# Narrowing float64 weights on chip: the low part as 16-bit integers behind the absolute values, and the first transposed copy between two quarters

## The chip, the cores and the metric

The kernel runs on one core of one Trainium2 chip. The metric is the device time of one execution in microseconds (us); the figure to be forecast is the median of several executions.

## The reference, cut to what matters

```python
def _attn_ref(q, k, v, g_norm):                 # q, k, v: (8, 8, 576, 64) float32
    kv = np.einsum('bhsd,bhse->bhde', k, v)
    out = np.einsum('bhsd,bhde->bhse', q, kv)
    rms = np.sqrt(np.mean(out * out, axis=-1, keepdims=True) + 1e-06)
    return (out / rms * g_norm).astype(np.float32)

def _moe_ref(x, w1, w2, w3, w_out):             # x: (4608, 512)
    a = x @ w1                                  # w1, w2: (512, 1024)
    b = x @ w2
    h = a * b @ w3                              # w3: (1024, 1024)
    return (h @ w_out).astype(np.float32)       # w_out: (1024, 512)
```

The four weight matrices arrive as float64, which the kernel receives as 64-bit integers; the attention inputs are float32. The rows of the attention output of all heads, side by side, are the `x` of the second part.

## The kernel before, in words

The kernel never forms `h`. It first computes the product `w3 @ w_out` once (1024 by 512, called the **fold** here) and then, for nine groups of 512 tokens, the gate products `a * b` and one product with the folded matrix. The fold is the first 80 us of the execution; the rest is the token groups.

No engine computes with float64, so every weight is first narrowed to float32 by `conversion`. Its two 32-bit words are read apart: `hi` and `lo`. ScalarE writes two things: the **low part** (L165), `lo * 2**-51 + 2.0` as a float32, so that the three bits that float32 can still hold end up in the lowest bits of the word, and the **absolute value** (L167), `|hi|` taken as if it were a float32. VectorE then does four operations: L169 overwrites the upper 16 bits of the low part with the sign and an exponent bit, taken from the top of `hi`; L173 clamps the absolute value; L176 shifts it left by three bits; L181 adds the low part to it. The low parts lie in two areas of the tile `ab`, taken in turn by the number of the conversion. `conversion` is a generator: its first two steps issue the ScalarE operations, the last the four of VectorE. `begin_next` takes the first two steps of every part of the next conversion, `end_next` the remaining ones and then issues the next load.

The loads (L207, SyncE's queue) bring one `raw` tile each: for the fold's chunk `c`, 128 columns of the first half of `w3` in its left half and 128 rows of `w_out` in its right half. There are four `raw` tiles, so the loads of the first four chunks go out at the start. Chunk 0 is loaded and converted in four quarters of 256 (two of `w3`, then two of `w_out`), chunks 1 to 5 in two halves of 512 each (`w3`, then `w_out`), the later ones whole.

Each chunk of `w3` must be transposed for TensorE: `turn_w3` does four TensorE transposes (L701) and one ScalarE copy (L703) into `ab`. Then `fold_chunk` (L717) multiplies: four matmuls 512 wide, one for each of four sums; for chunk 0 it is eight matmuls 256 wide, of which the second four need the last quarter. `keep_warm` (L287) multiplies the identity with itself, with no use of the result: `keep_warm(n, small)` does n matmuls 128 wide and then `small` matmuls 16 wide.

In this stretch the order on TensorE, VectorE, ScalarE and SyncE is the order in which the program issues, written out by hand (`manual_schedule`); afterwards VectorE and ScalarE are ordered by a scheduler. Before the change, the order at the start is: `keep_warm(11)`; all eight ScalarE operations of chunk 0; all of VectorE's; the transposes and the copy; `keep_warm(1, 21)`; the ScalarE operations of chunk 1; a small transpose of `g_norm`; then the loop over the chunks. In its first round it finishes chunk 1 on VectorE, multiplies chunk 0, and puts the copy of chunk 1 (`turn_w3(0, 1)`) between two ScalarE operations of chunk 2.

Conversions in the first token group carry `by_scalar`: there ScalarE also multiplies by `g_norm` (L133).

Of the kernel before, what the change touches and what calls it, by code (L numbers as in the profile page):

```python
# [14 lines left out]
U16 = mybir.dt.uint16  # L15
I64 = mybir.dt.int64
AF = mybir.ActivationFunctionType
# [5 lines left out]
def kernel(  # L23
# [32 lines left out]
    nc = tc.nc  # L56
# [27 lines left out]
    def bank(pool, tag):  # L84
        return pool.tile([P, 512], FP32, name=tag, tag=tag)
# [51 lines left out]
    def conversion(  # L137
        n, dst, raw, cols=slice(0, 1024), scale=None, by_scalar=False, in_parts=False
    ):

        dst, raw = (t if len(t.shape) == 3 else t[:, cols] for t in (dst, raw))
        if raw.dtype == FP32:
            yield
            yield
            if in_parts:
                yield
            nc.vector.tensor_copy(out=dst, in_=raw)
            if scale is not None:
                scale_by(dst, scale, by_scalar)
            return  # L150
        words = raw.bitcast(U32).rearrange("p (n w) -> p n w", w=2)
        lo, hi = words[:, :, 0], words[:, :, 1]

        low = ab[n % 2][:, NF // 2:].rearrange("p a i t -> p (a i t)")[:, cols]
        low_bits = low.bitcast(U32)

        low_top = low.bitcast(U16).rearrange("p (n w) -> p n w", w=2)[:, :, 1]
        hi_top = raw.bitcast(U16).rearrange("p (n w) -> p n w", w=4)[:, :, 3]
        if len(dst.shape) == 3:
            wide = dict(c=dst.shape[1])  # L160
            lo, hi, low, low_bits = (
                t.rearrange("p (c n) -> p c n", **wide) for t in (lo, hi, low, low_bits)
            )
        dst_bits = dst.bitcast(U32)
        nc.scalar.activation(low, lo, AF.Copy, scale=2.0 ** -51, bias=2.0)  # L165
        yield
        nc.scalar.activation(dst, hi.bitcast(FP32), AF.Abs)  # L167
        yield
        nc.vector.tensor_scalar(  # L169
            out=low_top, in0=hi_top, scalar1=0x8000, scalar2=0x4000,  # L170
            op0=ALU.bitwise_and, op1=ALU.bitwise_or,
        )
        nc.vector.tensor_scalar(  # L173
            out=dst, in0=dst, scalar1=LEAST, scalar2=MOST, op0=ALU.max, op1=ALU.min
        )
        nc.vector.tensor_scalar(  # L176
            out=dst_bits, in0=dst_bits, scalar1=3, scalar2=None, op0=ALU.logical_shift_left
        )
        if in_parts:
            yield  # L180
        nc.vector.tensor_tensor(out=dst_bits, in0=dst_bits, in1=low_bits, op=ALU.add)  # L181
        yield
        if scale is not None:
            scale_by(dst, scale, by_scalar)
# [61 lines left out]
    begun = []  # L246
    in_first_group = False

    def begin_next(between=None, at=1):

        if len(begun) < len(todo):
            begun.append(conversions(len(begun)))
            for n, (c, _) in enumerate((c, i) for c in begun[-1] for i in range(2)):
                if between is not None and n == at:
                    between()
                next(c)
# [8 lines left out]
    def all_of(steps):  # L265
        for _ in steps:
            pass
# [14 lines left out]
    def keep_warm(n, small=0):  # L282

        t = bank(ps_mm, "mm")
        for i in range(n + small):
            w = P if i < n else 16
            nc.tensor.matmul(t[0:w, 0:w], lhsT=ident[:, 0:w], rhs=ident[:, 0:w], start=True, stop=True)  # L287
# [409 lines left out]
    def turn_w3(half, c):  # L697
        t_ps = bank(ps_at, "at").rearrange("p (m f) -> p m f", m=NH)
        for m in range(NH):
            src = chunks[:, c, 0, m * P:(m + 1) * P]  # L700
            nc.tensor.transpose(t_ps[:, m, :], src, ident)  # L701

        nc.scalar.copy(place_w3(half, c), t_ps)  # L703
# [711 lines left out]
    with tc.manual_schedule(  # L1415
        engines={mybir.EngineType.DVE, mybir.EngineType.Activation, mybir.EngineType.SP}
    ):
        for _ in range(RAW):
            load_next()
        nc.scalar.activation(const.tile([P, 1], FP32, name="warm"), eps_col, AF.Sqrt)  # L1420
        g_row = const.tile([1, P], FP32, name="g_row")
        for e in range(2):
            nc.scalar.dma_start(
                out=g_row[:, e * D:(e + 1) * D], in_=g_norm.rearrange("(o d) -> o d", o=1)
            )


        keep_warm(11)
        begin_next()
        end_next()  # L1430
        turn_w3(0, 0)
        keep_warm(1, 21)
        begin_next()

        g_ps = bank(ps_at, "at")[:, 0:1]
        nc.tensor.transpose(g_ps, g_row, ident[0:1, 0:1])
        nc.scalar.copy(g_col, g_ps)
        for c in range(KF):

            if c > 2:  # L1440
                begin_next()
            end_next()
            if c == 4:
                load_four("k", 0, 0)
                load_q(0, 0)
            elif c == 5:
                load_four("v", 0, 0)
                load_q(0, 1)
                load_q_left(0)
            if c == 0:  # L1450
                for n in range(2):
                    fold_chunk(0, c, range(NH), slice(n * N, (n + 1) * N))
                begin_next(lambda: turn_w3(0, 1))
                keep_warm(2)
                continue
            fold_chunk(0, c, range(NH - 1))
            if c < 3:
                begin_next(lambda: turn_w3(0, c + 1), 2)
            else:
                turn_w3(*((0, c + 1) if c + 1 < KF else (1, 0)))  # L1460
            fold_chunk(0, c, [NH - 1])


        first = batch(0)
        first.start()
        BEGIN, PRODUCT = {1: 0, 4: 1}, {2: 0, 5: 1}
        norms = {}
        FIRST = len(converted) + KF - 1
        turns, SPLIT = {}, {0: 3, 2: 5, 4: 7}
        for c in range(KF):  # L1470
            if c in BEGIN:
                first.begin_q(2 * BEGIN[c], 2 * BEGIN[c] + 1)
                if c == max(BEGIN):
                    x_first = first.x_by_dma(0, nc.vector.tensor_copy, split=nc.scalar.copy)
                    next(x_first)
                    next(x_first)
                    all_of(turns[c + 1])
            if c - 1 in norms:
                all_of(norms[c - 1])
            if c < KF - 2:  # L1480
                if c < max(BEGIN):
                    begin_next()
                if c == max(BEGIN) + 1:
                    for steps_of_w in begun[len(converted)]:
                        next(steps_of_w)
                    all_of(x_first)
                else:
                    end_next(False)
                if c in SPLIT:
                    t = turns[SPLIT[c]] = w3_by_dma(SPLIT[c])  # L1490
                    next(t)
                    next(t)
                if len(raws) < FIRST:
                    load_next()
                if c == 2:
                    for steps_of_w in begun[len(converted)]:
                        next(steps_of_w)
                elif c == max(BEGIN):
                    run(sum_w(0))
            elif c == KF - 2:  # L1500
                end_next(False)
            fold_chunk(1, c, [0])
            if c in BEGIN:
                first.begin_kv(BEGIN[c])
                if c == max(BEGIN):
                    load_q_left(1)
            if c + 1 == KF:
                for r in range(2):
                    first.turn(2 + r)
                run(combine_x(0))  # L1510
                end_next(False)
                for _ in range(3):
                    load_next()
            fold_chunk(1, c, range(1, NH - 1))
            if c == 2:
                all_of(turns[c + 1])
            elif c + 1 < KF and c + 1 not in turns:
                turn_w3(1, c + 1)
            if c in (max(BEGIN), KF - 2):
                begin_next()  # L1520
            fold_chunk(1, c, [NH - 1])
            if c in PRODUCT:
                norms[c] = first.product(PRODUCT[c])
                next(norms[c])
                if c > max(BEGIN):
                    all_of(turns[c + 2])
                next(norms[c])
# [8 lines left out]
    for n, T in enumerate(groups):  # L1536
# [29 lines left out]
        if T in IN_TWO:  # L1566
            p = 2
# [141 lines left out]
```

## Time and profile before

| what | us |
|---|---|
| median of three executions (740.18, 740.49, 740.83) | 740.49 |
| the profiled execution's own time | 740.17 |
| its span, first to last instruction of the program | 738.3 |
| TensorE busy | 732.9 |
| VectorE busy | 628.8 |
| ScalarE busy | 379.2 |

The granted TensorE clock of the profiled execution is 1.00 throughout. PE is TensorE's matmul, PEld its weight load, DVE VectorE, ACT ScalarE, POOL GpSimd, SP SyncE; L12 is line 12 of the kernel. A float32 matmul has two records in the trace, a transpose one. A row of the timeline gives the start, the duration, the engine, the line, what is written and read, the shape, the count and, in brackets, how long the engine was idle before and what ended that.

### The profile page before, as it was taken

What the parts mean: (1) busy time and instruction counts of PE and PEld (TensorE: products, weight loads), DVE (VectorE), ACT (ScalarE), POOL (GpSimd) and SP (SyncE); (2) the same over time, 40 slices, a digit from 0 to 9 for tenths busy, and PEclk for the clock granted to TensorE, in tenths of its full rate; (3) what the DMA queues carried; (4) which work ended last, traced back from release to release, by engine and by line L of the source; (5) the groups of instructions that cost most, each with busy time, mean ns of one, the idle gap of its engine ahead of it and who ended that gap; (6) DMA issues with size and microseconds to landing.
All of it is one profiled execution on the core that took longest, in us unless ns stands there. A gap on an engine that the chain in (4) does not pass through costs nothing.

```text
span 738.3 us, 16923 instructions
## 1 busy us (share of the span) xinstructions
PE 732.9 (99%) x6867; PEld 658.7 (89%) x6867; DVE 628.8 (85%) x1259; ACT 379.2 (51%) x660; POOL 22.3 (3%) x29
## 2 busy tenths in 40 slices
PE   8999999999999999999999999999999999999998
PEld 6445788888899999999999999999999999999998
DVE  7988898968879689968996899689979987997797
ACT  7787778415652675257626762676177313212321
POOL 0000000221000000100000001000001000000000
PEclk9999999999999999999999999999999999999999
DMA  9999925599999698869987988698747662565354
GB/s 316 347 329 252 288 94 147 149 333 293 325 277 317 177 282 259 256 168 273 265 275 163 299 243 272 166 298 234 261 103 223 225 209 86 182 216 160 135 196 141
DMA packets 138769, 170.44 MB, mean 231 GB/s; under 512 B 81220, under 2 KB 114116, under 8 KB 138692
## 3 DMA queue, kind: packets, MB, share of 16 engines
q1 hardware_dynamic: 136240, 155.02, 70.7%
q10 hardware_dynamic: 2452, 14.35, 5.7%
q8 instruction: 54, 0.88, 0.5%
q14 instruction: 23, 0.19, 0.1%
HBM read 130.55 MB, written 20.71 MB: 205 GB/s over the span
## 4 chain that ended last, share of the span: by engine, by line
PE 98%; DVE 1%; DMA 1%; issue 0%; SPq 0%; ACT 0%
PE mm L748 38%; PE mm L1298 23%; PE mm L1040 21%; PE mm L717 7%; PE at L347 3%; PE at L748 2%; PE mm L425 1%; PE at L425 1%; DMA raw<-in_moe_w_out_dram 1%; PE at L701 1%; PE at L1341 0%; PE at L444 0%; PE at L367 0%; DVE ab L169 0%; DVE chunks L176 0%
## 5 line engine op out<-in xcount | busy, mean ns | idle before, releaser
L1089 ACT COPY slots<-mm 128x512 f32<-128x512 f32 x88 | 51.6, 586 | 126.8 <-PE mm L1298 83.7
L748 PE MATMUL mm<-xT,w_sb 128*128 128x256 f32 x448 | 102.9, 379 | 0.0
L748 PEld LDWEIGHTS mm<-xT,w_sb 128*128 128x128 f32 x448 | 84.4, 190 | 11.4 <-issue 0.5
L748 PE MATMUL mm<-xc,ws 128*128 128x256 f32 x336 | 76.1, 379 | 0.0
L748 PEld LDWEIGHTS mm<-xc,ws 128*128 128x128 f32 x336 | 63.9, 190 | 8.6
L766 ACT COPY slots<-mm 128x512 f32<-128x512 f32 x59 | 34.5, 585 | 69.6 <-PE mm L748 64.4
L717 PE MATMUL mm<-chunks,ab 128*128 128x512 f32 (+1 forms) x136 | 59.8, 578 | 0.4 <-DVE chunks L181 0.4
L1093 DVE TENSOR_TENSOR slots<-mm,slots 128x512 f32<-128x512 f32 x66 | 45.1, 684 | 17.2 <-PE mm L1040 17.0
L1090 ACT COPY slots<-mm 128x384 f32<-128x384 f32 x88 | 42.3, 481 | 25.8 <-PE mm L1298 23.0
L1040 PE MATMUL mm<-ws,w3o_sb 128*128 128x128 f32 x350 | 54.0, 275 | 0.0
L1298 PE MATMUL mm<-w3o_sb,ab 128*128 128x128 f32 x368 | 48.9, 276 | 0.0
L393 DVE TENSOR_REDUCE inv<-sq 128x8 f32<-128x512 f32 (+1 forms) x40 | 24.6, 630 | 26.6 <-ACT sq L392 26.6
L1040 PEld LDWEIGHTS mm<-ws,w3o_sb 128*128 128x128 f32 x350 | 46.4, 192 | 0.0
L1298 PEld LDWEIGHTS mm<-w3o_sb,ab 128*128 128x128 f32 x368 | 45.4, 192 | 0.6
L717 PEld LDWEIGHTS mm<-chunks,ab 128*128 128x128 f32 x136 | 23.6, 190 | 22.6 <-issue 15.5
L1298 PE MATMUL mm<-w3o_sb,raw 128*128 128x128 f32 x340 | 43.5, 275 | 0.0
L1298 PEld LDWEIGHTS mm<-w3o_sb,raw 128*128 128x128 f32 x340 | 40.7, 192 | 0.0
L748 PE MATMUL mm<-xc,w_sb 128*128 128x256 f32 x160 | 38.5, 384 | 0.0
L1094 DVE TENSOR_TENSOR slots<-mm,slots 128x384 f32<-128x384 f32 x66 | 36.4, 551 | 2.2 <-PE mm L1298 1.6
L748 PE MATMUL mm<-xT,ws 128*128 128x256 f32 x160 | 38.1, 381 | 0.0
L748 PEld LDWEIGHTS mm<-xT,ws 128*128 128x128 f32 x160 | 30.1, 190 | 4.3 <-ACT slots L766 0.2
L748 PEld LDWEIGHTS mm<-xc,w_sb 128*128 128x128 f32 x160 | 29.8, 190 | 4.2
(246 smaller groups left out, 1647.4 us busy)
## 6 DMA issues: line engine op xcount, KB each, us to landing
w3o_sb<-w_l SPq DMA_DIRECT2D x21, 896.0 KB, 6.0
w3o_sb<-w3o_l SPq DMA_DIRECT2D x18, 896.0 KB, 6.3
raw<-in_moe_w_dram SPq DMA_DIRECT2D x31, 512.0 KB, 7.8
raw<-w3o_l SPq DMA_DIRECT2D x15, 896.0 KB, 4.6
w3o_sb<-w3o_l ACTq DMA_DIRECT2D x14, 896.0 KB, 4.6
k_sb<-in_k_dram SPq DMA_DIRECT2D x16, 576.0 KB, 5.1
v_sb<-in_v_dram SPq DMA_DIRECT2D x16, 576.0 KB, 6.0
q_sb<-in_q_dram SPq DMA_DIRECT2D x32, 256.0 KB, 4.6
```

Of the source, the lines that this page charges most:

```text
L347: nc.tensor.matmul(ps[r * D:(r + 1) * D, :], lhsT=k_sb[rows, r, cols], rhs=v_sb[rows, r, cols], start=(j == 0), stop=(j == JS - 1),)
L393: adds["norm"] = nc.vector.tensor_reduce(out=inv[:, i], in_=sq.rearrange("p (h d) -> p h d", d=D), axis=AX.X, op=ALU.add)
L425: nc.tensor.matmul(o_ps[l][tokens, n * D:(n + 1) * D], lhsT=qT[r][rows, e, i, tokens], rhs=kv_b[rows, m // 2 ^ l, e, h, :], start=True, st ...
L717: nc.tensor.matmul(sums_ps[half][m][:, cols], lhsT=w3T[half, c][:, m, :], rhs=chunks[:, c, 1, cols], start=(c == 0 and cols.start == 0), s ...
L748: nc.tensor.matmul(ps[:, u, :], lhsT=lhsT(a_name, u, c), rhs=rhs(b_name, c),  start=(u == 0 and c == 0 and new), stop=(c == chunks - 1), s ...
L766: copies.setdefault(name, []).append(nc.scalar.copy(t, ps))
L1040: nc.tensor.matmul(ps[place // 4][:, place % 4, :], lhsT=x, rhs=y, start=new and place // 4 not in seen, stop=True, skip_group_check=True,)
L1089: nc.scalar.copy(z[:, 0:4], ps[0])
L1090: return nc.scalar.copy(z[:, 4:7], ps[1][:, 0:3])
L1093: nc.vector.tensor_add(z[:, 0:4], ps[0], z[:, 0:4])
L1094: nc.vector.tensor_add(z[:, 4:7], ps[1][:, 0:3], z[:, 4:7])
L1298: nc.tensor.matmul(ps[place // 4][:, place % 4, :], lhsT=x[:, c, :], rhs=y[:, c, :], start=new and place // 4 not in seen, stop=(c == 1), ...
```

## The change

It has three parts. Where `by_scalar` is not set, which is all of the fold's conversions and the weights converted during it, ScalarE does the absolute value first and the low part second, and writes the low part as `lo * 2**-29` in 16-bit integers into the lower half of each 32-bit word; VectorE's L169 still writes the upper halves. Chunk 0's steps are written out: ahead of the ScalarE operations of its last quarter come VectorE's operations of the first two quarters, the four transposes of `w3` and the copy. And five of the 21 small `keep_warm` matmuls ahead of chunk 0's product move to the place ahead of chunk 1's.

```diff
         low = ab[n % 2][:, NF // 2:].rearrange("p a i t -> p (a i t)")[:, cols]
         low_bits = low.bitcast(U32)
-        low_top = low.bitcast(U16).rearrange("p (n w) -> p n w", w=2)[:, :, 1]
+        low_halves = low.bitcast(U16).rearrange("p (n w) -> p n w", w=2)
+        low_bottom, low_top = low_halves[:, :, 0], low_halves[:, :, 1]
         hi_top = raw.bitcast(U16).rearrange("p (n w) -> p n w", w=4)[:, :, 3]
...
-        nc.scalar.activation(low, lo, AF.Copy, scale=2.0 ** -51, bias=2.0)
-        yield
+        if by_scalar:
+            nc.scalar.activation(low, lo, AF.Copy, scale=2.0 ** -51, bias=2.0)
+            yield
         nc.scalar.activation(dst, hi.bitcast(FP32), AF.Abs)
         yield
+        if not by_scalar:
+            nc.scalar.activation(low_bottom, lo, AF.Copy, scale=2.0 ** -29)
+            yield
         nc.vector.tensor_scalar(
             out=low_top, in0=hi_top, scalar1=0x8000, scalar2=0x4000,
             op0=ALU.bitwise_and, op1=ALU.bitwise_or,
...
         keep_warm(11)
-        begin_next()
+        quarters = conversions(0)
+        begun.append(quarters)
+        for n, steps_of_w in enumerate(quarters):
+            if n == 3:
+                for done_first in quarters[0:2]:
+                    all_of(done_first)
+                turn_w3(0, 0)
+            next(steps_of_w)
+            next(steps_of_w)
         end_next()
-        turn_w3(0, 0)
-        keep_warm(1, 21)
+        keep_warm(1, 16)
         begin_next()
...
                 begin_next(lambda: turn_w3(0, 1))
-                keep_warm(2)
+                keep_warm(2, 5)
                 continue
```

Compared instruction by instruction, the two programs issue the same operations on every engine in the same order except for these: the two ScalarE operations of each such conversion change places, the copy L703 of chunk 0 stands ahead of the last quarter's two ScalarE operations, and the five small matmuls stand later. L169 no longer waits for ScalarE, and the add L181 now does. SyncE's queue and GpSimd are unchanged.

More of the change, by code (lines that the diff above doesn't have):

```diff
@@ L160, in conversion @@
             wide = dict(c=dst.shape[1])
-            lo, hi, low, low_bits = (
-                t.rearrange("p (c n) -> p c n", **wide) for t in (lo, hi, low, low_bits)
+            lo, hi, low_bottom, low_bits = (
+                t.rearrange("p (c n) -> p c n", **wide) for t in (lo, hi, low_bottom, low_bits)
             )
         dst_bits = dst.bitcast(U32)
-        nc.scalar.activation(low, lo, AF.Copy, scale=2.0 ** -51, bias=2.0)
-        yield
+        if by_scalar:
+            nc.scalar.activation(low, lo, AF.Copy, scale=2.0 ** -51, bias=2.0)
+            yield
         nc.scalar.activation(dst, hi.bitcast(FP32), AF.Abs)
         yield
+        if not by_scalar:
+            nc.scalar.activation(low_bottom, lo, AF.Copy, scale=2.0 ** -29)
+            yield
         nc.vector.tensor_scalar(
```

## The prediction

> **What bounds the kernel now.** I read the page first: the busy times and the chain that ended last.
>
> ```profile
> PE 732.9 (99%) x6867; PEld 658.7 (89%) x6867; DVE 628.8 (85%) x1259; ACT 379.2 (51%) x660; POOL 22.3 (3%) x29
> ...
> PE 98%; DVE 1%; DMA 1%; issue 0%; SPq 0%; ACT 0%
> ```
>
> TensorE holds 98% of the chain; all that the change touches is in the rest. The chain in order of time (first 100 us; start, duration) shows where TensorE takes over for good:
>
> ```profile
> 1.75 4.99 DMA raw<-in_moe_w_out_dram
> ...
> 7.24 0.31 DVE ab L169
> ...
> 12.98 0.70 DVE chunks L181
> 13.68 0.14 issue
> 13.82 2.81 PE mm L717 x6
> ```
>
> Until 13.82 us the end is set by a load, then by VectorE's conversions. At 13.82 TensorE begins chunk 1's product, and every later piece of the chain up to 100 us is TensorE. From one matmul record to the next, a 512 wide one takes 0.43 us; after 13.82 the only wait in the fold is one of 0.05 us, ahead of chunk 2 at 17.82 (the record before starts at 17.34). So what the change is worth is how far it moves 13.82, plus at most that 0.05. The timeline before it:
>
> ```profile
> 6.77 0.44 ACT L165 ACTIVATE ab<-raw 128x256 f32<-128x256 uint32 x1 [1.11 <-DMA raw<-in_moe_w_out_dram]
> ...
> 7.24 0.31 DVE L169 TENSOR_SCALAR ab<-raw 128x256 uint16<-128x256 uint16 x1 [0.46 <-ACT ab L165]
> ...
> 7.56 0.29 DVE L173 TENSOR_SCALAR chunks<-chunks 128x256 f32<-128x256 f32 x1
> ...
> 8.18 0.57 ACT L703 COPY ab<-at 128x512 f32<-128x512 f32 x1
> ...
> 12.99 0.58 ACT L703 COPY ab<-at 128x512 f32<-128x512 f32 x1 [0.52 <-PE at L701]
> 13.48 0.68 ACT L167 ACTIVATE chunks<-raw 128x512 f32<-128x512 f32 x1
> ```
>
> The third quarter's data land at 6.74. VectorE stands idle 0.46 us for the low part, and its clamp L173, which is what the result needs next, can only start at 7.56. From there VectorE has no gap up to 13.67.
>
> **The change, part by part.** *The swap.* VectorE's steps, start to start, from rows where nothing waits: a quarter 0.20 (L169, 8.56 to 8.76), 0.33, 0.33 and 0.34 us for the add up to the next L169; a half 0.34 (11.72 to 12.06), 0.46, 0.46 and 0.61. With the absolute value first, L169 runs as soon as the data land, beside ScalarE, and the clamp follows 0.03 after the absolute value (0.42 long). The low part comes 0.34 after the absolute value's start and ends before the add, two VectorE steps later, needs it. Step by step:
> - Quarter 0: absolute value 3.60 to 4.02, clamp 4.05, add 4.71 (before: 5.05).
> - Quarter 1, whose data are there at 4.89: absolute value to 5.31, clamp 5.34, add 6.00 to 6.43 (before: 6.35).
> - Quarter 2: 6.77 to 7.19, clamp 7.22, add 7.88 to 8.31 (before: 8.21).
> - Quarter 3: L169 8.22, clamp 8.42, add 9.08 (before: 9.41).
> - Chunk 1, first half: L169 9.42, clamp 9.76, add 10.68. Its absolute value (data at 8.90) ends at 9.57, so the 0.09 that L173 waited for ScalarE at 10.18 goes too (before: 11.11).
> - Second half: L169 11.29, add 12.55 to 13.24 (before: 12.98 to 13.67).
>
> The matmul followed the add's end by 0.15, so chunk 1's product starts at 13.39: **0.43 us earlier**. With VectorE ahead, chunk 2's add ends 0.6 earlier or more, and the wait of 0.05 there goes: **0.48 us** in all.
>
> *The copy between two quarters.* Quarter 1's add ends at 6.43, so the last two transposes run from 6.48 to 6.92 (0.44 as at 6.83). ScalarE, behind quarter 2's low part (7.10), starts the copy at 7.43 and ends it at 8.00 instead of 8.75. TensorE's first product then waits for quarter 2's add alone: 8.36 instead of 8.80. Queued behind the copy are quarter 3's two ScalarE operations: 0.49 after the copy's start (12.99 to 13.48), so 7.92, the absolute value ends at 8.34 and the clamp could go at 8.37, while VectorE itself reaches it at 8.42. The copy costs nothing, under a cover of 0.05 us. ScalarE does hold what stands behind a copy: chunk 2's absolute value, whose data had landed by 11.78, started at 13.48, behind the copy of 12.99. The Trainium skill, page "TensorE: Matmul & The Clock Gate", architectural detail, says that ScalarE's queue is a strict first-in first-out; by it the quarter waits until 7.92 as reckoned, without it 7.48, and the sum is the same by either, as VectorE is busy till 8.42.
>
> What could be late next? Chunk 0's product takes 3.56 us to its end as before (8.80 to 12.36): 11.92. Chunk 1's transposes need the first half's add (ended 11.37) and run to 12.52; the copy 12.55 to 13.14, ahead of 13.39 by 0.25. Data limit nothing: the second half's are read at 10.25 in the trace, VectorE wants them at 11.29.
>
> *The five small matmuls.* At 0.05 us each (42 records from 7.42 to 8.46), 21 of them ended just ahead of the product; 16 end about 8.0, under the wait to 8.36. Five more after chunk 1's transposes end near 13.2, under the wait to 13.39. Cost nothing on either side; if that cover is gone, at most 0.25 us.
>
> *Unknown prices.* An activation that writes 16-bit integers from 32-bit ones is not in the trace. Nearest rows (by form, first 100 us):
>
> ```profile
> L165 ACT ACTIVATE ab<-raw 128x1024 f32<-128x1024 uint32 x13 | 15.1, 1163 | 0.0
> ...
> L320 ACT COPY ab<-chunks 128x1024 uint16<-128x1024 uint16 x3 | 3.5, 1181 | 0.0
> ...
> L306 ACT COPY xT<-xn 128x1024 uint16<-128x1024 uint16 x2 | 2.0, 1053 | 0.0
> ```
>
> From 10% less to 2% more; I take no change, as L320 too writes half words with a step. The add now waits for ScalarE as well as for VectorE. Dependent VectorE operations show 0.02 of issue between them in the chain; a second such step on six adds is 0.12 us, while six L169 lose one. I take nothing and keep 0.12 less or more for the range.
>
> The sum: 738.3 - 0.48 span, 740.17 - 0.48 = 739.69 for an execution like the profiled one. The median lies 0.32 above that execution, so the forecast is **740.0 us**. That is 0.06%; about 0.2% is what a measurement of this kernel can tell from no change.
>
> **Rivals.** *The copy takes the place of the wait removed.* With a cover of 0.05 us, every further delay of the copy passes through quarter 3's clamp into VectorE's row of work. If quarter 1's transposes come at 7.0 instead of 6.48, the copy ends at 8.5, the clamp starts at 8.87 and 0.45 is given back: 740.4 to 740.5. For it: ScalarE waited 7.9 us in nine places for transposes to end. Against: here the transposes end 0.5 before ScalarE gets to the copy. Chance 0.12.
>
> *Integer writes are slow, and ScalarE becomes the bound.* A chunk of the fold takes TensorE 3.95 us (21.07 to 25.02 in the chain). ScalarE needs for it four operations at 0.59 and a copy at 0.48, 2.84 in all. It decides once a half's low part takes over 1.15 us instead of 0.59, 1.9 times. At double the price the last quarter and the two halves of chunk 1 each wait for ScalarE, and chunk 1's product starts at about 14.25 by the same step sum, 0.43 later than now; chunk 2 adds some 0.5, and from 40 to 80 us, where ScalarE is busy 33.1 of 40 us, six low parts of 1.16 more fill it, for 0 to 2 us. That gives 741.5 to 743.5, say 742.3, slower. Against: the rows above. The Trainium skill, page "ScalarE: Activation LUTs", section on the table load's cost, says 186 ns and 0.833 ns an element with immediates for every function, float32 and bfloat16 alike, which speaks against a doubling; integers it does not mention there. Chance 0.03.
>
> *More is gained than summed.* VectorE's work from quarter 2's landing (6.74) on is two quarters at 1.20 and two halves at 1.87, so chunk 1 cannot start before 13.0: at most 0.8 us, 739.7. Chance 0.05.
>
> **How the numbers follow.** Forecast 0.80, the rivals 0.12, 0.03 and 0.05. The three executions before spread by 0.65 us around their median. The forecast with its unknown of 0.12 and half that spread gives 739.6 to 740.4; the first rival and the spread above it reach to 740.9, the third below to 739.4. Over 0.2%, 1.5 us, no gain can go, since TensorE has no other wait to lose; I leave 0.03 for a disturbance of the measurement. Slower by that much is the second rival and as much disturbance, 0.04; the rest, 0.93, is within.
>
> **What would show it.** Right: chunk 1's first product near 13.4, L169 of quarter 2 at 6.77 with no wait for ScalarE, L703 of chunk 0 near 7.43, no gap on VectorE from 8.4 to 13.2, TensorE without gaps from there. Wrong: a low part over 0.5 us for 256 columns; VectorE idle ahead of quarter 3's L173 or ahead of an add; a product later than 13.6; or a later wait on TensorE that takes the 0.4 us back.

## The result and the profile after

| | median, us | executions | span of the profiled one |
|---|---|---|---|
| before | 740.29 | 15 | 738.3 |
| after | 741.42 | 15 | 740.5 |

The changed kernel is **slower by 1.1 us**: the ratio is 1.0016, with a 95% interval from 1.0009 to 1.0022. The forecast was 740.0 us, 739.4 to 740.9, so the measured time lies above the range and on the other side of no change.

The page of the changed kernel: busy times, and the split of the chain that ended last.

```profile
PE 733.9 (99%) x6867; PEld 658.5 (89%) x6867; DVE 627.2 (85%) x1259; ACT 381.8 (52%) x660; POOL 22.5 (3%) x29
...
PE 90%; DVE 6%; ACT 2%; DMA 1%; issue 1%; DVEq 0%; ACTq 0%
```

The busy times have hardly moved. The chain has: TensorE held 98% of it and now holds 90%, VectorE went from 1% to 6%. The chain of the first 100 us in order of time (start, duration, what) says where. The changed kernel's lines are, on ScalarE, L169 for the absolute value and L172 for the low part; on VectorE, L174 for the upper halves (L169 before), L178 for the clamp, L181 for the shift and L186 for the add; L706 and L708 for the transposes and their copy, L722 for the products.

```profile
4.41 0.30 DVE chunks L181
4.71 0.03 issue
4.76 0.09 issue
4.85 0.42 DVE chunks L186
...
31.00 1.24 DVE chunks L186
32.24 0.14 issue
32.38 0.63 PE at L706 x4
...
37.48 1.16 ACT chunks L169
38.63 1.25 ACT ab L172
39.89 1.40 ACT w3o_sb L728 x3
41.29 0.50 ACT ab L708
41.79 0.04 issue
41.83 2.84 PE mm L722 x6
```

In the kernel before, this chain passed to TensorE at 13.82 us and stayed there. Now VectorE's own row of conversions sets the end from 4 us right up to 32.38, and ScalarE's row sets it once more at 41.83 (and again at 61.87). Ahead of every add (L186) stand two pieces of issue, 0.03 and 0.09, where the kernel before had one of 0.02. The groups by form of VectorE's first 33 us (count, then busy us, mean ns of one, and idle us just before them), first of before, then of after:

```profile
L181 DVE CUSTOM_DVE_ANT_0 chunks<-chunks,ab 128x1024 uint16<-128x1024 uint16 x10 | 6.9, 692 | 0.3
```

```profile
L186 DVE CUSTOM_DVE_ANT_0 chunks<-chunks,ab 128x1024 uint16<-128x1024 uint16 x10 | 6.9, 693 | 1.4
```

The add itself lasts as long as before; the idle time ahead of ten of them went from 0.3 to 1.4 us, 0.03 to 0.14 each. In the trace a separate wait instruction of 0.02 stands in that gap. It waits for VectorE's own shift (L181), and only behind it does the add go out, which itself waits for ScalarE. A half takes VectorE 1.97 us from add to add (10.51 to 12.48) instead of 1.87.

ScalarE's groups by form, first 100 us, are the second thing that moved:

```profile
L172 ACT ACTIVATE ab<-raw 128x1024 uint16<-128x1024 uint32 x10 | 13.7, 1366 | 0.0
L172 ACT ACTIVATE ab<-raw 128x512 uint16<-128x512 uint32 x10 | 7.7, 772 | 0.0
```

Before, the same low parts took 1163 and 682 ns as float32: the 16-bit integers cost 17% and 13% more, 0.20 us for a whole one.

The start, from the timeline:

```profile
6.01 0.43 ACT L169 ACTIVATE chunks<-raw 128x256 f32<-128x256 f32 x1 [0.33 <-DMA raw<-in_moe_w_out_dram]
...
7.10 0.59 ACT L708 COPY ab<-at 128x512 f32<-128x512 f32 x1 [0.27 <-PE at L706]
...
13.32 1.10 PE L722 MATMUL mm<-chunks,ab 128*128 128x512 f32 x2
```

Chunk 1's product starts at 13.32 instead of 13.82. The 0.50 us are there, and by 32.38 they are gone.

One thing in this execution is its own. A load that the kernel before has too was late, and TensorE waited 1.28 us for it:

```profile
221.95 7.03 DMA raw<-w3o_l
228.98 0.14 issue
229.11 6.49 PE mm L1303 x56
```

Of the thirteen traces of this case it shows in one other, of a kernel whose other ten executions do not have that time (739.28 to 740.82 us beside 741.24). It explains why the profiled execution took 742.35 us and not 741.4; it does not explain the median. The steps below are therefore read from a second trace of the changed kernel.

### The profile page after: what moved, and what is told of

Read it like the earlier page. It is cut to its first block, busy times and chain, and to the rows that moved or that the text cites. A ratio compares the mean times of both kernels' runs of the same rounds, so it can differ in the third digit from the quotient of the medians.

```text
span 740.5 us, 16915 instructions
## 1 busy us (share of the span) xinstructions
PE 733.9 (99%) x6867; PEld 658.5 (89%) x6867; DVE 627.2 (85%) x1259; ACT 381.8 (52%) x660; POOL 22.5 (3%) x29
## 4 chain that ended last, share of the span: by engine, by line
PE 90%; DVE 6%; ACT 2%; DMA 1%; issue 1%; DVEq 0%; ACTq 0%
PE mm L753 36%; PE mm L1303 22%; PE mm L1045 20%; PE mm L722 4%; PE at L352 3%; PE at L753 2%; DVE chunks L186 1%; PE mm L430 1%; DMA raw<-w3o_l 1%; PE at L430 1%; DVE chunks L181 1%; DVE ab L174 1%; DVE chunks L178 1%; PE at L1346 0%; DMA raw<-in_moe_w_dram 0%
## 5 line engine op out<-in xcount | busy, mean ns | idle before, releaser
L722 PE MATMUL mm<-chunks,ab 128*128 128x512 f32 (+1 forms) x136 | 59.9, 578 | 0.4 <-ACT ab L708 0.2
L722 PEld LDWEIGHTS mm<-chunks,ab 128*128 128x128 f32 x136 | 23.6, 190 | 22.6 <-issue 15.5
```

What stands on the lines that cost most here:

```text
L722: nc.tensor.matmul(sums_ps[half][m][:, cols], lhsT=w3T[half, c][:, m, :], rhs=chunks[:, c, 1, cols], start=(c == 0 and cols.start == 0), s ...
```

## The experiments

Three theories stood at the outset, and a fourth came up as traces were read. **W**: the wait that the add L186 gained makes VectorE's row longer by 0.10 us per conversion, and the first whole conversion, chunk 6, comes too late. **I**: the integers make ScalarE late, and nothing else matters. **P**: a later stretch or a load loses the time. **F**: the change took 15 wait instructions out of ScalarE's program (931 to 916 records in the trace), and so moved other instructions to places in it where they start late. Medians below are of 11 executions (33 or 27 of the kernel before on the same chip), in us; the offset is how much later TensorE starts an instruction than in the first trace of before.

**The changed kernel again.**

> The changed kernel once more, for a second trace. Three theories are told apart in this series. Theory W (the second wait): the add L186 now waits for ScalarE too, and each add starts 0.137 us after the shift instead of 0.033; over the fifteen adds up to chunk 6's that is 1.6 us on VectorE's row of work, which eats the 0.5 us gained at the start, and chunk 6's transposes, which had 0.10 us to spare, wait. Theory I (integers): the 16-bit write makes ScalarE's low part 17% longer and that alone is the loss. Theory P (phase): the fold is not the cause; what is lost is lost after 100 us, at loads that land late. W and I: TensorE 0.4 to 0.5 us behind the kernel before at 97 us, mostly from chunk 6's transposes at 32 us; the load at 222 us that took 7.0 us in the first trace is back near 5, so the time is 741.2 to 741.6. P: a wait of over 1 us for a load again, at 228 us or another place.

741.31 against 740.35, ratio 1.0013 (1.0004 to 1.0022); span 739.2, no wait for a load. TensorE's offset goes in steps: -0.32 from chunk 1's product on, -0.05 at chunk 2's (the wait of before, gone), +0.14 at 25.48 (chunk 4's product, which waits for the copy L708), +0.46 at 32.54 (chunk 6's transposes), +0.14 at 42.0 and +0.20 at 62.0 (each time the copy L708 again), +0.31 up to 435, nearly all of it between 427 and 435. The sum is +0.88; the spans differ by 0.9. So these five places of loss hold the whole of it, and P in its form of a load falls.

**Each part alone.** `swap_only` is the changed `conversion` with the start of the kernel before; `start_only` is the reverse.

```diff
 # swap_only, against after
-        quarters = conversions(0)
...
-        keep_warm(1, 16)
+        begin_next()
+        end_next()
+        turn_w3(0, 0)
+        keep_warm(1, 21)
...
-                keep_warm(2, 5)
+                keep_warm(2)
```

> The first part of the change alone: conversion as changed, with the start sequence and the small matmuls of the kernel before. W: chunk 1's product starts near 13.4 (VectorE sets it), chunk 6's transposes wait as in the changed kernel; 741.0 to 741.6. I: the same. If instead the copy between the quarters were the loss, 740.0.

> The second and third part of the change alone: the start sequence with the copy between the quarters and the small matmuls as changed, the conversion as before. VectorE sets the start of chunk 1's product here (13.8 us), and nothing of the copy is on its row of work. All theories: 740.2 to 740.6, no change, no wait above 0.15 us on TensorE at 32 us.

`swap_only`: 741.36 against 740.35, ratio 1.0014 (1.0006 to 1.0023), with the same steps at 25.79 (+0.13), 32.87 (+0.48), 42.3 (+0.14), 62.3 (+0.18) and 427 to 435 (+0.30). Its chunk 1 product started at 13.82, as before the change and not near 13.4 as expected. `start_only`: 740.28 against 740.30, ratio 0.9997 (0.9989 to 1.0006), without a step over 0.05 behind chunk 1's product. The conversion is the whole loss; the copy between two quarters costs nothing, and brings nothing that these medians can tell.

**The integers without the wait.** The low part stays 16 bits wide, but ScalarE writes it first and the absolute value second. VectorE's clamp then waits for ScalarE's last operation, and the add needs no wait for ScalarE.

```diff
         if by_scalar:
             nc.scalar.activation(low, lo, AF.Copy, scale=2.0 ** -51, bias=2.0)
-            yield
+        else:
+            nc.scalar.activation(low_bottom, lo, AF.Copy, scale=2.0 ** -29)
+        yield
         nc.scalar.activation(dst, hi.bitcast(FP32), AF.Abs)
         yield
-        if not by_scalar:
-            nc.scalar.activation(low_bottom, lo, AF.Copy, scale=2.0 ** -29)
-            yield
```

> As the changed kernel, 16-bit low part included, but ScalarE writes the low part first and the absolute value second, as before the change; the add then needs no wait of its own for ScalarE. W: the step from shift to add is 0.033 us again, chunk 1's product starts near 13.8, chunk 6's add ends near 32.1, no wait above 0.15 us there; the longer ScalarE operations may still cost 0.1 to 0.4 us at the copies near 41 and 61 us; 740.4 to 740.8. I: as slow as the changed kernel, 741.2 to 741.6. P: no forecast below 741.

740.64 against 740.35, ratio 1.0006 (0.9997 to 1.0015). Its chain of waits (here L169 is the low part, L171 the absolute value, L705, L707 and L721 the transposes, copy and products):

```profile
25.22 3.64 PE mm L721 x8
28.85 0.44 PE at L705 x4
29.29 3.52 PE mm L721 x8
32.81 0.44 PE at L705 x4
33.25 3.52 PE mm L721 x8
...
37.72 1.38 ACT ab L169
39.10 0.99 ACT chunks L171
40.09 1.45 ACT w3o_sb L727 x3
41.54 0.49 ACT ab L707
42.03 0.04 issue
42.08 2.84 PE mm L721 x6
```

At 32.81 TensorE runs without a wait: chunk 6 is in time again, though this execution's start was 0.25 us *later* than before's. At 42.08 TensorE still waits for ScalarE's copy, and at 62.08 too: steps of 0.15 and 0.18 us. A third one, of 0.12, lies inside the first line: the eight matmul records from 25.22 last 3.64, where the chain of before has `25.02 3.52 PE mm L717 x8`, and the third of them, chunk 4's first, waits for the copy. These 0.45 us are the integers' own price. The step at 427 us is gone as well. W and I are thus told apart: the one holds 32 us, the other 25, 42 and 62.

**The wait moved: chunk 6 in two halves.** W says that what decides at 32 us is that chunk 6 comes in one piece.

```diff
-        cuts = range(0, 1025, 256 if i == 0 else 512 if i < 6 else 1024)
+        cuts = range(0, 1025, 256 if i == 0 else 512 if i < 7 else 1024)
```

> The changed kernel with chunk 6 converted in two halves of 512 instead of whole, so that its w3 half is ready some 1.4 us earlier; five more VectorE operations' fixed cost, about 0.5 us, falls on chunk 7. Theory W with the late place at chunk 6: the wait of 0.5 us on TensorE at 32 us is gone; a smaller one of 0.1 to 0.3 us may come at chunk 7 near 36 us; TensorE at 97 us 0.2 to 0.4 us ahead of the changed kernel's, total 740.9 to 741.2. If the wait at 32 us comes from something else (a load, ScalarE): it stays, 741.3 to 741.5.

740.86 against 740.30, ratio 1.0008 (0.9999 to 1.0017). There is no step at 32 us, and chunk 7, now the first whole one, has it instead (chain of waits):

```profile
35.16 1.24 DVE chunks L186
36.40 0.14 issue
36.53 0.64 PE at L706 x4
```

That is a step of +0.44 in the offset, more than the 0.1 to 0.3 expected. The place moved with the first whole conversion, as W says; that loss stayed. The median is lower than the changed kernel's all the same, as the step at 427 us is missing here.

**Float32 low parts behind the absolute value.** The order of the change (absolute value first) with the format of before. L169's step (the line of before: VectorE's upper halves) must then follow the low part. In `float_late_top` it stands between shift and add, in `float_mid_top` between clamp and shift; in both the add waits for VectorE alone. `float_mid_old_start` is the latter with the start of before, `float_mid_again` a repeat.

```diff
 # float_mid_top, against after
         if not by_scalar:
-            nc.scalar.activation(low_bottom, lo, AF.Copy, scale=2.0 ** -29)
+            nc.scalar.activation(low, lo, AF.Copy, scale=2.0 ** -51, bias=2.0)
             yield
-        nc.vector.tensor_scalar(out=low_top, in0=hi_top, ...)
         nc.vector.tensor_scalar(out=dst, in0=dst, scalar1=LEAST, scalar2=MOST, ...)
+        nc.vector.tensor_scalar(out=low_top, in0=hi_top, ...)
         nc.vector.tensor_scalar(out=dst_bits, in0=dst_bits, scalar1=3, ...)
```

> As the changed kernel, absolute value first, but the low part is a float32 again (scale 2**-51, bias 2.0), written second, and VectorE's order is clamp, shift, L169's step, add: the wait for ScalarE falls on L169's step, which needs nothing from the shift, and the add waits for VectorE alone. W: start near 13.2 to 13.4, no wait at 32 us, 739.7 to 740.0, faster than the kernel before by 0.3 to 0.6 us. I: the same figure, as the integers are gone. P: 740.8 or more.

> As float_late_top, but VectorE's order is clamp, L169's step, shift, add, so that L169's step fills the gap that the shift leaves behind the clamp: a half should take 1.75 us on VectorE (0.34 + 0.34 + 0.46 + 0.61) instead of 1.87 before and 1.97 in the changed kernel. Chunk 1's product starts near 13.1 to 13.4 by the landing of the first loads, TensorE never waits after it, and the total is 739.6 to 739.9, faster than the kernel before by 0.4 to 0.8 us. If L169's step has to wait for ScalarE's low part, the half stays at 1.9 us and the total at 740.0.

> The float32 low part second, VectorE's order clamp, upper halves, shift, add, with the start of the kernel before. Theory W (a second wait on the add costs 0.10 us each time): no second wait, no step at 32 us, none at 42, 62 or 424. If the start's new order is what brings chunk 1's product from 13.8 to 13.35, it stands at 13.6 to 13.8 here and the time is 740.1 to 740.3; if the order of the four VectorE steps alone brings it, it stands at 13.35 and the time is 739.8.

> The version with the float32 low part second and the new start once more, to see whether it stands below the kernel before: 739.8 us, ratio 0.9993, chunk 1's product at 13.3 to 13.6 depending on when the second quarter's load lands, and no later step of TensorE.

| kernel | median | before | ratio | 95% |
|---|---|---|---|---|
| float_late_top | 740.02 | 740.35 | 0.9998 | 0.9989 to 1.0007 |
| float_mid_top | 739.76 | 740.30 | 0.9994 | 0.9985 to 1.0003 |
| float_mid_again | 740.02 | 740.22 | 0.9999 | 0.9990 to 1.0008 |
| float_mid_old_start | 740.06 | 740.22 | 0.9999 | 0.9990 to 1.0008 |

None shows a step at 25, 32, 42, 62 or 427 us. The chain of `float_mid_top` is TensorE's through all of them:

```profile
28.47 3.52 PE mm L722 x8
31.99 0.44 PE at L706 x4
32.43 3.52 PE mm L722 x8
35.95 0.44 PE at L706 x4
```

A half takes VectorE 1.90 us in `float_late_top` (add to add, 11.22 to 13.12) and 1.74 in `float_mid_top` (10.76 to 12.51): in the latter neither the clamp, nor L169's step, nor the shift depends on its neighbour, and each starts 0.08 to 0.11 before the one ahead ends. `float_mid_top` is the best version found. It lies 1.3 to 1.7 us below the changed kernel (741.31 and 741.42). In both runs it also lies below the kernel before, by 0.54 and 0.20, but both intervals hold 1, so it is not shown to be faster than that one. `float_mid_old_start` has chunk 1's product at 13.92 and `float_mid_again` at 13.70: the expected 13.6 to 13.8 and 13.3 to 13.6 were each missed by 0.1, and the two medians do not tell the starts apart. `float_late_top` has it at 13.96, 0.6 behind what was expected.

**ScalarE's instruction places.** The step at 427 us needs the chain of `swap_only` near it:

```profile
424.47 0.61 DVE ab L1131
425.08 0.02 issue
425.11 0.02 ACTq L771
425.12 0.32 issue
425.44 0.28 ACT slots L771
```

VectorE is done at 425.08, ScalarE's wait instruction ends at 425.12, and the copy behind it starts 0.32 us later with nothing else to wait for. Between such a wait and its copy there are otherwise 0.04. ScalarE's records hold three gaps of this kind in the changed kernel, each of 0.32 or 0.33 us: records 319, 575 and 831 (from 0), 256 apart. The kernel before has them at 319 and 831, on other instructions. To test it, tiny ScalarE copies (128 by 1) were put ahead of chunk 7's conversion, where ScalarE waits for TensorE anyway, four of them and then one.

```diff
+            if c == 6:
+                for n in range(1):      # 4 in pad4
+                    nc.scalar.copy(pad_col[:, n:n + 1], eps_col)
             if c > 2:
                 begin_next()
```

> The changed kernel with four copies of one column added on ScalarE ahead of chunk 7's conversion, where ScalarE waits about 1 us for TensorE. They shift all later instructions of ScalarE by four places. In the traces every 256th instruction of ScalarE (places 320, 576, 832) starts 0.28 to 0.33 us late; the change removed 15 wait instructions on ScalarE, which put place 576 on a copy at 424 us that TensorE waits for (+0.31 us there in both traces with the second wait, none in the three kernels with the old count). Theory F (place in the instruction stream): no step at 424 to 435 us, the fold as in the changed kernel, total 0.3 us less than it, 741.0 to 741.1. If that step is a load or the later phase: it stays, 741.3.

> The changed kernel with one tiny ScalarE copy (128 by 1) added ahead of chunk 7's conversion, where ScalarE waits for TensorE anyway. Theory F (place in ScalarE's instruction stream): the place 576 moves from the copy that TensorE waits for at 424 us onto the wait instruction ahead of it, which lies in ScalarE's idle time, so the step of 0.3 us between 424 and 435 us goes, the other steps (0.45 to 0.55 at 32, 0.17 at 42, 0.17 to 0.2 at 62) stay: 741.0 us. Rival (the step at 424 belongs to the order or to the loads of the changed kernel and not to the place): it stays at 0.3, 741.3 us.

`pad4`: 741.10 against 740.30, ratio 1.0012 (1.0004 to 1.0021). `pad1`: 741.28 against 740.22, ratio 1.0018 (1.0009 to 1.0027). The timelines of `swap_only` and of `pad1`, ScalarE alone, show what one inserted instruction does to that copy:

```profile
425.44 0.58 ACT L771 COPY slots<-mm 128x512 f32<-128x512 f32 x1 [1.43 <-DVE ab L1131]
```

```profile
425.42 0.59 ACT L771 COPY slots<-mm 128x512 f32<-128x512 f32 x1 [1.16 <-DVE ab L1131]
```

Its idle time falls from 1.43 to 1.16; the gap behind its wait instruction is 0.04 in `pad1` instead of 0.32. The step between 427 and 435 falls from 0.30 to 0.05 in `pad1` and to 0.07 in `pad4`, which in turn has a new one of 0.19 at 76 us (its cause stays open). With `six_in_halves` (one instruction more as well, no step) the trace bears F out. The time does not: `pad1` was to be 741.0 and was 741.28. Its profiled execution (741.33) has the quarter loads late and chunk 1's product at 14.02, 0.53 behind that of the repeat of the changed kernel; chunk 6's transposes then start at 33.09, 0.55 behind. That is more than the 0.3 saved. Whether its other executions were late in the same way, the trace of one cannot tell.

## Why the prediction was wrong

**Right.** Chunk 1's product came at 13.32 (predicted 13.39). The copy cost what its cover allowed: it ended at 7.69, and quarter 3's clamp started 0.26 behind L174 (7.79 to 8.05) instead of 0.20, so 0.06 us. It was held by the transposes (idle 0.27 for them), not by ScalarE's low part. That is the first rival's mechanism, at far less than the 0.45 it was priced at: the cover of 0.05 gave way in this execution. In the repeat it held (8.04 to 8.24). Chunk 1's product did not feel the small matmuls. The wait of 0.05 at chunk 2 went, as predicted.

**But 13.39 was hit by two errors that cancel.** Quarter 2's data landed at 6.01 instead of 6.77, and every add stood 0.10 further back. The repeat shows the term alone: quarter 2 there began at 6.46, 0.31 earlier than the 6.77 of the prediction. The predicted step sum would give 13.08; four adds lie between (quarters 2 and 3, the halves of chunk 1), 4 x 0.103 = 0.41, so 13.49. The trace has 13.49. The same sum gives 13.55, 13.60, 13.82 and 14.02 for `six_in_halves`, `pad4`, `swap_only` and `pad1`, where quarter 2 began at 6.52, 6.57, 6.79 and 6.99; their traces have 13.54, 13.60, 13.82 and 14.02. So with quarter 2's data at 6.77, as predicted, the start would have gained next to nothing: the four second waits cost 0.41 of the 0.43 that the swap brought, and what the traces of the changed kernel show as a lead is the earlier load. That the number came close was luck.

**The step that failed first: the second wait on the add.** The text priced it by issue rows between dependent VectorE operations, 0.02 each, and counted six adds: 0.12, in the range but not in the sum. The measured price is 0.103 (a gap of 0.137 ahead of the add instead of 0.034), five times that, and the adds that count are fifteen, up to chunk 6, not six: 1.5 us of VectorE's row. The count stopped where the prediction took TensorE to have taken over. The rows that were used are of an operation that waits for VectorE alone. Here the added condition makes a separate instruction, and that one waits for the operation just ahead, so it cannot be done early. Trace rows of before with a separate wait (L169's at 28.20 and 30.88) cost nothing, as they wait for loads, while the add ahead still runs. The Trainium skill, page "Perfetto Trace Analysis", section on identifying dependency chains, says that an instruction which waits for several engines may have separate semaphore instructions put ahead of it; the trace agrees, with the two pieces of issue of 0.03 and 0.09 in place of one of 0.02, and the wait instruction between them.

**The second: "TensorE has no other wait to lose".** No wait is not the same as much slack. The prediction looked for waits behind 13.82 and found one of 0.05; a second of 0.08, ahead of 41.62, it overlooked (the chain of before has eight matmul records from 40.84 on for 3.62 instead of 3.52 us). And it did not look for how late each add ended before TensorE wanted it. The timelines of before, VectorE and TensorE, have it:

```profile
30.86 1.23 DVE L181 CUSTOM_DVE_ANT_0 chunks<-chunks,ab 128x2048 uint16<-128x2048 uint16 x1
```

```profile
32.34 0.60 PE L701 MATMUL at<-ident,chunks 128*128 128x128 f32 x4
```

The add ends at 32.09, and a transpose can follow 0.15 later, at 32.24: a slack of 0.10. VectorE's row to there grew by 9 x 0.10 behind chunk 1, less the 0.26 that it had lost at chunk 2 before and lost no more: 0.6 us, more than the lead of 0.50. In the first trace chunk 6's add ended 0.14 later than before's. Because this place is set by VectorE's row, the earlier product of chunk 1 could not pay for it: whatever TensorE was ahead, it waited for at 32.38.

**The third: the integers' price.** From "10% less to 2% more" the prediction took no change, by the row L320, a copy that writes half words with a step. That row has 16-bit input too; an activation from 32-bit words to 16-bit integers took 17% more. Ahead of the copies at 25, 41 and 61 us ScalarE had next to nothing to spare: the copy ended at 25.65, 41.57 and 61.38 in before, TensorE's product started at 25.72, 41.62 and 61.43. One whole low part stands ahead of each of the last two, 0.20 longer, and TensorE lost 0.14 and 0.20. Ahead of the first stand three halves' low parts, with which ScalarE took 4.11 us from copy to copy (20.74 to 24.85) instead of 3.98 (21.11 to 25.09), and TensorE lost 0.14. The rival on slow integers asked for 1.9 times the price before it would decide. That holds for ScalarE as the bound of a whole chunk. For a wait it takes the slack of one place, which here was next to none. The Trainium skill, page "ScalarE: Activation LUTs", section on the table load's cost, gives one rate for float32 and bfloat16 alike; for 16-bit integers this trace shows another, 1366 ns against 1163.

**The fourth was not considered:** 15 waits fewer on ScalarE moved every later instruction 15 places forward in its program, and 0.31 us were lost 390 us behind the change.

| term | predicted | trace of the repeat |
|---|---|---|
| start, to chunk 1's product | -0.43 | -0.32, by the load alone |
| wait at chunk 2 | -0.05 | -0.05 |
| second wait on the add, felt at chunk 6 | 0 (0.12 either way) | +0.46 |
| integers, three copies | 0 | +0.48 |
| ScalarE's places | not considered | +0.31 |
| sum | -0.48 | +0.88 |

The two terms in the middle are not independent: chunk 6's place is set by VectorE's row, so the 0.14 at 25.48 would without the integers have been lost at 32.54. The forecast's base was high as well: the median lay 0.32 above the profiled execution with three executions, 0.12 with fifteen. Of the prediction's own signs of being wrong, the last came true: a later wait on TensorE that takes the gain back. The slower rival had the wrong mechanism: not one price doubled, but three small ones on rows without slack. Why the medians put the loss at 0.96 and 1.13 where this trace has 0.88 is not shown; the starts spread by as much: in the thirteen traces ScalarE begins with the second quarter's data between 4.35 and 5.38 us, and with the third's between 6.01 and 6.99, whatever the kernel.

## What to carry to other kernels

An engine that shows no waits may have another engine a tenth of a microsecond behind it. Before a change that lengthens a row, even by little, list for each hand-over how early the other side was, far beyond the place of the edit, and multiply the small price by all the repetitions up to the tightest one. When two producers are reordered, put the new wait on an instruction that does not follow an operation of its own engine on which it depends: the same four VectorE operations took 1.97, 1.90, 1.87 or 1.74 us, by their order and waits alone.

## What the runs showed of the hardware

- A second wait cost 0.10 us on VectorE where the separate wait instruction waits for the operation just ahead on the same engine (gap 0.137 instead of 0.034), and nothing where its condition was met while that operation ran (28.20 and 30.88 in before).
- An activation from 32-bit integers to 16-bit integers, written into every other half word, took 1366 ns for 1024 columns and 772 for 512; to float32 1163 and 682.
- On ScalarE single instructions started about 0.28 us late (0.32 behind their wait instruction instead of 0.04) at fixed places of its program: records 319, 575 and 831 of the changed kernel, 703 in `pad1` and `six_in_halves`. All distances are multiples of 128. What happens there was not measured; that adding one instruction ahead moves it was.
- The third quarter's data were taken between 6.01 and 6.99 us in the traces; from 13.32 to 14.02 lay chunk 1's product in the five traces that share the changed start.
